# Windowed attention into a gated MLP on one core: gates without tanh, exponentials shifted by their bias, another first load and another order of the work

## The chip, the cores and the metric

The kernel runs on one core of a Trainium2 chip. The metric is the device time of one execution in microseconds (us); the number given for the kernel before is the median of three runs.

## The reference, cut to what matters

```python
q, k, v: (4, 8, 768, 64) float32          # batch, heads, sequence, head width
scores = q @ k^T / 8                      # per batch and head
keep   = (key < 4) | (0 <= query - key < 128)        # 4 sink keys and a window of 128
a      = softmax(where(keep, scores, -1e9))
x      = (a @ v) as (3072 tokens, 512)
h      = x @ w_in                         # 512 -> 2048
g      = h * sigmoid(1.702 * h)
out    = g @ w_out                        # 2048 -> 512, float32
```

## The kernel before

The tokens are cut into 24 blocks of 128 (six for each batch entry). A query block sees its own 128 keys up to the diagonal, those of the block ahead of it above the diagonal, and four sink keys. Two blocks make a group; there are 12 groups.

For a block, in order: the queries and keys are loaded by POOL's queue as float16 (`qkn`; block 0's first as float32 by SP's queue, `rawq` and `rawk`, and cast by ACT) and transposed (`qkT`; blocks 0 to 7 by PE into a `tq` tile, which DVE or ACT copies out, the later ones by a DMA transpose of SP's queue, both blocks of a group at once). PE makes the scores with the own keys (`own`), with those of the block before (`prv`) and with the sinks (`snk`). DVE packs `prv` into the masked half of `own`, takes the row maxima (`mx`), subtracts them (`e32`), and ACT takes the exponentials (`a16`). These are transposed, in blocks 0 to 3 by PE (`ta`, copied to `at`), later by a DMA transpose of SP's queue. POOL then splits them into `at` and `atp` by two selects. PE multiplies with the values (`av`), DVE divides by the sums (`xn`), and the result is transposed to `xT`, in blocks 0 to 3 by PE (`tx`), later by a DMA transpose. For a group, PE makes eight tiles of `h` (`hT`), ACT turns each into a gate (`gT`), and PE multiplies them with `w_out` (`o`, four parts for each of two token blocks), after which ACT or DVE copies to `osb` and SP's queue stores.

Group 0 is done apart. Its eight `hT` tiles are split by token block (four tiles each), so that the first four need block 0 alone. Its gates are made as (1 + tanh(0.851 h)) * h: ACT takes tanh, which lies in the same function table as exp, into `th`, and DVE multiplies. From group 1 on ACT takes the gate in one instruction, whose function lies in another table, so that ACT loads a table ahead of the gates and again ahead of the next exponentials.

In blocks 0 to 3 one half of each block (`nb` = 1) is not subtracted by DVE: ACT reads the scores in PSUM and subtracts the maximum by the bias of the exponential, head by head, in four instructions of 128 columns.

Nothing here is ordered by the Python loops. Every step is put into a list (`Plan.add`) with a cost, its dependences and the buffer rings that it takes and gives back (`RING`: among them two PSUM buffers `own`, three `mm`, which `tq`, `ta`, `tx`, `hT`, `o` and the `own` of blocks 1 and 3 share). `Plan.run` goes through the list with these costs, engine by engine, always taking the free step of the lowest key; the keys stand in the table `KEYS`. The order in which the steps are taken is the order of the instructions on each engine, and each engine works through its own in that order.

Of the kernel before, what the change touches and what calls it, by code (L numbers as in the profile page):

```python
# [11 lines left out]
FP32 = mybir.dt.float32  # L12
# [7 lines left out]
P = 128  # L20
# [11 lines left out]
    nb={0: 1, 1: 1, 2: 1, 3: 1},  # L32
# [3 lines left out]
    tanh=(0,),  # L36
# [6 lines left out]
    sel2=(),  # L43
    steady=8,
# [196 lines left out]
def kernel(  # L241
# [32 lines left out]
    plan = Plan(RING)  # L274

# [22 lines left out]

    def hw(key, cost, fn, xfer, **kw):
# [3 lines left out]
    o_bias0 = hw(-98, 0.4, lambda: nc.sync.dma_start(bias0, bias0_d.ap()), 0.1)  # L303
    o_later = hw(-97, 0.4, lambda: nc.sync.dma_start(later, later_d.ap()), 0.1)
    o_bias1 = hw(-96, 0.4, lambda: nc.sync.dma_start(bias1, bias1_d.ap()), 0.1)
    o_kept = hw(-94.5, 0.4, lambda: nc.sync.dma_start(kept, kept_d.ap()), 0.1)
    o_own = hw(-95, 0.4, lambda: nc.sync.dma_start(ownm, own_d.ap()), 0.1)
# [14 lines left out]
    def sw(key, cost, fn, xfer, **kw):  # L322
        return plan.add(POOL, key, cost, fn, xfer=xfer, post=2.6, **kw)
# [12 lines left out]

    def load_block(which, b, key, after=0.0):
        bb, r = divmod(b, 6)
        i = b % 2
        src = {"q": q, "k": k, "v": v}[which][bb, :, r * P : (r + 1) * P, :].rearrange("h s d -> s h d")  # L340
        if which == "v":
            return sw(key, 0.88, lambda: nc.gpsimd.dma_start(v65[:, b, :, 0:D], src), 1.0, deps=[z_1], after=after)  # L342
        w = "qk".index(which)
        buf = qkn[b // 2]
        if b in CFG["f32"]:
            raw = const.tile([P, H, D], FP32, name=f"raw{which}{b}")
            o_raw = hw(-120 + w, 0.4, lambda: nc.sync.dma_start(raw, src), 0.9)
            return plan.add(
                {DVE: 0.45, ACT: 0.6}, -95 + w, 0, lambda e: copy(e, buf()[:, i, w], raw), deps=[o_raw], take=[buf]
            )  # L350
        return sw(
            key, 0.88, lambda: nc.gpsimd.dma_start(buf()[:, i, w], src), 0.9,  # L352
            take=[buf], after=after,
        )
# [70 lines left out]
    o_qkt, o_ks, o_own_s, o_x = {}, {}, {}, {}  # L425

    for b in range(NBLK):
# [8 lines left out]
        if b in CFG["tq"]:  # L436
# [8 lines left out]
            for w in range(2):  # L445
                a = plan.add(
                    PE, K0 - 48 + w, 0.45 if b < 2 else 0.35, lambda w=w, f=t_qk: f(w), deps=[ld["qk"[w] + str(b)], o_ident],
# [37 lines left out]
        snk = ps("mi", (P, 4, 2, 4), FP32, f"snk{b}")  # L485
# [18 lines left out]
        if b in CFG["pemask"]:  # L504
            s_msk = plan.add(
                PE, K0 - 41, 0.9 if b == 0 else 0.43, lambda own=own, f=masks: f(own), deps=[o_bias0, o_identb] + (o_qkt[b] if b else []), take=own,
                slack=slack["s"],
            )
        s_own = None if both else plan.add(
            PE, K0 - 40, 0.5 if b < 2 else 0.24, lambda b=b, own=own, f=scores: f(own, b),  # L510
# [26 lines left out]
        if r > 0:  # L537

            def sinks(b=b, bb=bb, snk=snk):
                for j in range(4):  # L540
                    nc.tensor.matmul(snk()[:, j], qk_of(b)[:, j], ksb[:, bb, j], start=True, stop=True)

            s_snk = plan.add(PE, K0 - 40, 0.15, sinks, deps=([s_own] if b >= CFG['steady'] else []) + o_qkt[b] + [o_ks[bb]], take=[snk], give=[qkt[g]], slack=slack["s"])
# [69 lines left out]
        for l in range(2):  # L613
            if l >= 2 - nb:

                def exps(l=l, own=own, a16=a16, nbias=nbias):
                    for j in range(4):
# [7 lines left out]
                        ACT, K0 - 36.5, 1.02, exps, deps=[o_nb, z_a[b % RING["a16"]]],  # L625
# [18 lines left out]
        if r > 0:  # L644
# [9 lines left out]
            subs.append(plan.add(DVE, K0 - 38.7, 0.15, sub_s, deps=[top], take=[e32], give=[snk]))  # L654
# [99 lines left out]
        else:  # L754
            o_exp = plan.add(
                ACT, K0 - 36, 1.02, lambda a16=a16, e32=e32, w=w, f=exp: f(a16, e32, 0, w),
                deps=subs + zero, take=[a16], give=[e32], table="exp", slack=slack["e"],
            )
# [3 lines left out]
                deps=[o_exp], take=[at], give=[a16], xfer=1.35, post=0.8,  # L762
# [49 lines left out]
        if b in CFG["tx"]:  # L812
# [6 lines left out]
            o_tx = plan.add(PE, K0 - 28, 0.35, t_x, deps=norms, take=[tpx], give=[xn])  # L819
# [108 lines left out]
    order = plan.run()  # L928
    with tc.manual_schedule():
        for op in order:  # L930
            op.emit(op.on) if len(op.eng) > 1 else op.emit()
# [35 lines left out]
```

## Time and profile before

| | |
|---|---|
| median of the runs | 240.04 us (239.17 to 246.06, three runs) |
| profiled execution | 240.28 us, span 238.6 us |
| busy in the span | PE 216.5, DVE 141.2, ACT 133.8, POOL 114.2 us |
| chain that ended last | PE 76%, DMA 10%, DVE 7%, ACT 3% |
| moved by DMA | 33.38 MB, 126672 of 134152 packets under 512 bytes |

Busy times are those of one execution. Matmuls overlap each other, so PE's busy time says how long it had something in flight, not that it worked at its peak. The rows of a timeline give the start and the busy time in us, the engine, the line, the tiles with their shapes, the count, and in brackets how long the engine had been idle before and what ended that. SPq is the issue of DMAs by SP.

### The profile page before, as it was taken

What the parts mean: (1) busy time and instruction counts of PE and PEld (TensorE: products, weight loads), DVE (VectorE), ACT (ScalarE), POOL (GpSimd) and SP (SyncE); (2) the same over time, 40 slices, a digit from 0 to 9 for tenths busy, and PEclk for the clock granted to TensorE, in tenths of its full rate; (3) what the DMA queues carried; (4) which work ended last, traced back from release to release, by engine and by line L of the source; (5) the groups of instructions that cost most, each with busy time, mean ns of one, the idle gap of its engine ahead of it and who ended that gap; (6) DMA issues with size and microseconds to landing.
All of it is one profiled execution on the core that took longest, in us unless ns stands there. A gap on an engine that the chain in (4) does not pass through costs nothing.

```text
span 238.6 us, 5359 instructions
## 1 busy us (share of the span) xinstructions
PE 216.5 (91%) x2173; PEld 152.6 (64%) x2173; DVE 141.2 (59%) x344; ACT 133.8 (56%) x203; POOL 114.2 (48%) x130
## 2 busy tenths in 40 slices
PE   0368899899977999999999999999999999999994
PEld 0237598777436758648659568578577685685763
DVE  4279989827934556788598639767676571120000
ACT  3256686577226665737837565565666648351521
POOL 8878689199505618619708449644051210700000
PEclk9999769999999999999999999999999999999999
DMA  8999999999999997999999999999992223530202
GB/s 115 182 161 192 199 200 179 138 127 115 133 157 256 149 152 140 149 195 161 140 171 171 163 204 178 143 180 173 124 206 47 49 64 69 145 91 0 88 3 88
DMA packets 134152, 33.38 MB, mean 140 GB/s; under 512 B 126672, under 2 KB 131184, under 8 KB 134128
## 3 DMA queue, kind: packets, MB, share of 16 engines
q0 software_dynamic: 77024, 13.37, 73.8%
q1 hardware_dynamic: 57104, 19.67, 46.0%
q8 instruction: 17, 0.28, 0.5%
q14 instruction: 7, 0.06, 0.1%
HBM read 27.49 MB, written 6.29 MB: 142 GB/s over the span
## 4 chain that ended last, share of the span: by engine, by line
PE 76%; DMA 10%; DVE 7%; ACT 3%; SPq 1%; issue 1%; ACTq 0%; DVEq 0%
PE hT L852 33%; PE o L903 29%; DMA xT<-xn 7%; DMA bias<-cbias 3%; PE av L788 2%; PE av L792 2%; PE av L782 2%; PE own L522 2%; DVE mx L577 2%; DVE own L565 1%; DVE gT L873 1%; PE prv L522 1%; DVE xn L804 1%; DVE e L632 1%; PE ta L727 1%; PE tq L442 1%
## 5 line engine op out<-in xcount | busy, mean ns | idle before, releaser
L852 PE MATMUL hT<-xT,w_in 128*128 128x256 f16 (+1 forms) x832 | 93.5, 265 | 2.6 <-DMA xT<-xn 2.2
L903 PE MATMUL o<-w_out,gT 128*128 128x512 f16 (+1 forms) x400 | 90.2, 371 | 0.0
L852 PEld LDWEIGHTS <-w_in 128*128 128x128 f16 x832 | 74.6, 98 | 15.9 <-DMA xT<-xn 3.2
L882 ACT ACTIVATE gT<-hT 128x512 f16<-128x512 f32 x88 | 51.8, 597 | 41.7 <-PE hT L852 41.6
L676 POOL TENSOR_SCALAR_AFFINE_SELECT atp<-at 128x1024 f16<-128x1024 f16 (+1 forms) x23 | 22.5, 979 | 89.0 <-DMA at<-a 76.8
L903 PEld LDWEIGHTS <-gT 128*128 128x128 f16 x400 | 36.9, 98 | 35.0
L565 DVE COPY_PREDICATED own<-later,prv 128x512 f32<-128x512 uint16 x40 | 26.0, 691 | 18.0 <-PE prv L522 17.2
L577 DVE TENSOR_REDUCE mx<-own 128x4 f32<-128x512 f32 x48 | 31.1, 683 | 2.0 <-PE own L497 1.9
L664 ACT ACTIVATE a<-e 128x1056 f16<-128x1056 f32 (+3 forms) x27 | 24.5, 918 | 13.8 <-DVE e L632 6.8
L632 DVE TENSOR_TENSOR e<-own,mx 128x512 f32<-128x512 f32 x44 | 28.7, 682 | 0.5
L329 DVE COPY osb<-o 128x512 f32<-128x512 f32 (+1 forms) x7 | 4.6, 654 | 32.6 <-PE o L903 30.3
L333 ACT COPY osb<-o 128x512 f32<-128x512 f32 (+1 forms) x16 | 9.1, 572 | 25.8 <-PE o L903 25.8
L670 POOL TENSOR_SCALAR_AFFINE_SELECT at<-at 128x1024 f16<-128x1024 f16 (+1 forms) x23 | 22.4, 972 | 1.6
L342 POOL DMA_DIRECT2D v<-in_v_dram x24 | 21.7, 913 | 0.0
L352 POOL DMA_DIRECT2D qkn<-in_q_dram x23 | 21.0, 911 | 1.1 <-POOLq L948 0.8
L804 DVE TENSOR_TENSOR xn<-av,rcp 128x256 f16<-128x256 f32 x48 | 20.4, 425 | 1.7
L352 POOL DMA_DIRECT2D qkn<-in_k_dram x23 | 20.6, 898 | 0.3 <-DMA qkn<-in_q_dram 0.2
L803 DVE RECIPROCAL rcp<-av 128x4 f32<-128x4 f32 x48 | 8.4, 176 | 18.0 <-PE av L792 17.2
L788 PE MATMUL av<-v,at 128*128 128x65 f16 x192 | 17.5, 198 | 0.1
L788 PEld LDWEIGHTS <-at 128*128 128x128 f16 x192 | 14.9, 100 | 1.3
L442 PE MATMUL tq<-ident,qkn 128*128 128x128 f16 x64 | 7.6, 282 | 8.8 <-DMA ident<-cident 8.8
L792 PE MATMUL av<-v,atp 128*128 128x65 f16 x160 | 15.4, 197 | 0.0
(57 smaller groups left out, 180.7 us busy)
## 6 DMA issues: line engine op xcount, KB each, us to landing
out_dram<-osb SPq DMA_DIRECT2D x23, 256.0 KB, 2.6
v<-in_v_dram POOLq DMA_DIRECT2D x24, 128.0 KB, 6.2
qkn<-in_q_dram POOLq DMA_DIRECT2D x23, 128.0 KB, 6.3
qkn<-in_k_dram POOLq DMA_DIRECT2D x23, 128.0 KB, 5.7
w_in<-in_moe_w_in_dram POOLq DMA_DIRECT2D x4, 512.0 KB, 8.6
w_out<-in_moe_w_out_dram POOLq DMA_DIRECT2D x4, 512.0 KB, 11.2
at<-a SPq DMA_TRANSPOSE x20, 3.5
rawk<-in_k_dram SPq DMA_DIRECT2D x1, 256.0 KB
```

Source lines behind the costliest of these rows:

```text
L352: key, 0.88, lambda: nc.gpsimd.dma_start(buf()[:, i, w], src), 0.9,
L565: nc.vector.copy_predicated(out=own[l](), mask=later.unsqueeze(1).to_broadcast((P, 4, P)), data=prv[l]())
L577: lambda l=l, own=own, small=small: nc.vector.tensor_reduce(out=small[:, l], in_=own[l](), axis=AX.X, op=ALU.max),
L632: nc.vector.tensor_tensor(out=e32()[:, 512 * l : 512 * l + 512].rearrange("p (j s) -> p j s", j=4), in0=own[l](), in1=small[:, l].unsqueez ...
L664: nc.scalar.activation(out=a16()[:, lo:hi], in_=e32()[:, lo:hi], func=AF.Exp, scale=scale)
L670: nc.gpsimd.affine_select(out=dst()[:, lo : lo + n], in_=at()[:, lo : lo + n], pattern=[[0, n], [1, P]], compare_op=ALU.is_ge, fill=0.0, b ...
L676: nc.gpsimd.affine_select(out=dst()[:, lo : lo + n], in_=at()[:, lo : lo + n], pattern=[[0, n], [-1, P]], compare_op=ALU.is_gt, fill=0.0, ...
L788: nc.tensor.matmul(av()[:, j], ato()[:, c], v65[:, b, h], start=(r == 0), stop=(r == 0))
L804: nc.vector.tensor_tensor(out=xn()[:, i].rearrange("p (j l) d -> p l j d", l=2)[:, l], in0=av()[:, :, 0:D], in1=rcp.unsqueeze(2).to_broadc ...
L852: nc.tensor.matmul(ht()[:, n], w_in16[:, c, bass.ts(f, P)], xt[g]()[:, tok, c], start=(c == 0), stop=(c == 3))
L882: lambda fs=fs, cols=cols, gt=gt, ht=ht: nc.scalar.activation(out=gt()[:, fs[0] : fs[-1] + 1, cols], in_=ht(), func=AF.Gelu_apprx_sigmoid),
L903: nc.tensor.matmul(po(), gt()[:, F, bass.ts(t, P)], w_out16[:, F, cols], start=(F == 0), stop=(F == NF - 1))
```

## The change

- Group 0's gates are no longer made by tanh: ACT takes them by the gate function, in two batches of four, each after a table load.
- In blocks 0 to 3 both halves (`nb` = 2) are shifted by the bias of the exponentials. DVE's subtraction remains for the sinks.
- `rawq` is the first DMA of SP's queue and `rawk` one of ACT's queue, ahead of ACT's first table load. The constants follow on SP's queue (`ident`, `bias0`, `later`, `bias1`, `ownm`); `kept`, which no step of this configuration reads, is no longer loaded.
- Where the plan leaves PE idle within its first 45 us, products of a zero tile (`fill`, 128 x 256) into an unused part of the sinks' PSUM bank are put: 15 ahead of everything, 23 more in seven places up to block 4's sinks.
- Some costs given to the plan are altered, and the table `KEYS` is another, so that the order differs on every engine and in every group. On PE, `hT0_3` now stands right after half of block 3's transposes, ahead of block 3's scores, and the group 0 products with `w_out` end ahead of group 1's first `hT`. On ACT, the first four gates stand between the exponentials of block 1 and of block 2, the last four between those of block 3 and of block 4. On POOL, three loads more (block 8's keys, values and queries) are issued ahead of block 4's selects, and the four parts of `w_in` are its 3rd, 7th, 10th and 11th load, where they were the 4th, 12th, 14th and 18th. On SP, the order around group 2 is as before: block 4's and 5's `at`, `qkT` of blocks 8 and 9, `xT` of group 2, then block 6's and 7's `at`.

```diff
-    nb={0: 1, 1: 1, 2: 1, 3: 1},
+    nb={0: 2, 1: 2, 2: 2, 3: 2},
...
-    tanh=(0,),
+    tanh=(),
...
+    fill=(1.5, 45.0, 0.15, 0.11),
+    chain=99,
+    gap=3,
...
 KEYS = [ ... ]          # another table of the same kind
...
+    misc = psp.tile([P, 512], FP32, tag="mi", bufs=1, name="misc")
...
-    o_ident = hw(-99, 0.4, lambda: nc.sync.dma_start(ident, ident_d.ap()), 0.1)
...
-    o_kept = hw(-94.5, 0.4, lambda: nc.sync.dma_start(kept, kept_d.ap()), 0.1)
+    raw, o_raw = {}, {}
+    for b in CFG["f32"]:
+        for w, e in (("q", nc.sync), ("k", nc.scalar)):
+            src = {"q": q, "k": k}[w][b // 6, :, b % 6 * P : b % 6 * P + P, :].rearrange("h s d -> s h d")
+            raw[w, b] = const.tile([P, H, D], FP32, name=f"raw{w}{b}")
+            o_raw[w, b] = hw(-3000, 0.4, lambda dst=raw[w, b], src=src, e=e: e.dma_start(dst, src), 0.7)
+    o_ident = hw(-2000, 0.4, lambda: nc.sync.dma_start(ident, ident_d.ap()), 0.1)
...
+    fill = const.tile([P, 2 * P], FP16, name="fill")
+    z_f = plan.add(DVE, -2000, 0.1, lambda: nc.vector.memset(fill, 0.0))
...
-        snk = ps("mi", (P, 4, 2, 4), FP32, f"snk{b}")
+        snk = Buf("mi", lambda: misc[:, 0:32].rearrange("p (j l s) -> p j l s", l=2, s=4))
...
     order = plan.run()
+    idle, last = {}, 1.0
+    if CFG["fill"]:
+        lo, hi, rest, one = CFG["fill"]
+        for op in order:
+            if op.on == PE:
+                a, z = max(last, lo), min(op.start, hi)
...
+                idle[op] = max(0, int((z - a - rest) / (one if a > 6.0 else 2 * one)))
+                last = op.end
     with tc.manual_schedule():
         for op in order:
+            for n in range(idle.get(op, 0)):
+                nc.tensor.matmul(misc[:, 256:512], fill[:, 0:P], fill, start=True, stop=True)
             op.emit(op.on) if len(op.eng) > 1 else op.emit()
```

More of the change, by code (lines that the diff above doesn't have):

```diff
@@ L335, with load_one @@
     ld, qkn = {}, {}
+    late = []
     def load_block(which, b, key, after=0.0):
+        deps = [late[-CFG["gap"]]] if b >= CFG["chain"] and len(late) >= CFG["gap"] else []
+        op = load_one(which, b, key, after, deps)
+        if b >= CFG["chain"]:
+            late.append(op)
+        return op
+    def load_one(which, b, key, after, deps):
         bb, r = divmod(b, 6)
@@ L341, in load_block @@
         if which == "v":
-            return sw(key, 0.88, lambda: nc.gpsimd.dma_start(v65[:, b, :, 0:D], src), 1.0, deps=[z_1], after=after)
+            return sw(key, 0.88, lambda: nc.gpsimd.dma_start(v65[:, b, :, 0:D], src), 1.0, deps=[z_1] + deps, after=after)
         w = "qk".index(which)
@@ L345, in load_block @@
         if b in CFG["f32"]:
-            raw = const.tile([P, H, D], FP32, name=f"raw{which}{b}")
-            o_raw = hw(-120 + w, 0.4, lambda: nc.sync.dma_start(raw, src), 0.9)
             return plan.add(
-                {DVE: 0.45, ACT: 0.6}, -95 + w, 0, lambda e: copy(e, buf()[:, i, w], raw), deps=[o_raw], take=[buf]
+                {DVE: 0.45, ACT: 0.6}, -95 + w, 0, lambda e: copy(e, buf()[:, i, w], raw[which, b]),
+                deps=[o_raw[which, b]], take=[buf],
             )
@@ L352, in load_block @@
             key, 0.88, lambda: nc.gpsimd.dma_start(buf()[:, i, w], src), 0.9,
-            take=[buf], after=after,
+            take=[buf], after=after, deps=deps,
         )
@@ L423, in qk_of @@
         return qkt[b // 2]()[:, b % 2]
-    o_qkt, o_ks, o_own_s, o_x = {}, {}, {}, {}
+    o_qkt, o_ks, o_x, o_snk, o_sub = {}, {}, {}, {}, {}
     for b in range(NBLK):
@@ L446 @@
                 a = plan.add(
-                    PE, K0 - 48 + w, 0.45 if b < 2 else 0.35, lambda w=w, f=t_qk: f(w), deps=[ld["qk"[w] + str(b)], o_ident],
+                    PE, K0 - 48 + w, 0.45 if b < 2 and not CFG["fill"] else 0.27, lambda w=w, f=t_qk: f(w), deps=[ld["qk"[w] + str(b)], o_ident],
                     take=[tp], give=[qkn[g]],
@@ L505 @@
             s_msk = plan.add(
-                PE, K0 - 41, 0.9 if b == 0 else 0.43, lambda own=own, f=masks: f(own), deps=[o_bias0, o_identb] + (o_qkt[b] if b else []), take=own,
+                PE, K0 - 41, 0.9 if b == 0 and not CFG["fill"] else 0.43, lambda own=own, f=masks: f(own), deps=[o_bias0, o_identb] + (o_qkt[b] if b else []), take=own,
                 slack=slack["s"],
@@ L509 @@
         s_own = None if both else plan.add(
-            PE, K0 - 40, 0.5 if b < 2 else 0.24, lambda b=b, own=own, f=scores: f(own, b),
+            PE, K0 - 40, 0.5 if b < 2 and not CFG["fill"] else 0.24, lambda b=b, own=own, f=scores: f(own, b),
             deps=o_qkt[b] + [s_msk], take=[] if s_msk else own, give=[qkt[g]], slack=slack["s"] if s_msk is None else 0.0,
@@ L541, in sinks @@
                     nc.tensor.matmul(snk()[:, j], qk_of(b)[:, j], ksb[:, bb, j], start=True, stop=True)
-            s_snk = plan.add(PE, K0 - 40, 0.15, sinks, deps=([s_own] if b >= CFG['steady'] else []) + o_qkt[b] + [o_ks[bb]], take=[snk], give=[qkt[g]], slack=slack["s"])
+            s_snk = o_snk[b] = plan.add(PE, K0 - 40, 0.15, sinks, deps=([s_own] if b >= CFG['steady'] else []) + o_qkt[b] + [o_ks[bb]], take=[snk], give=[qkt[g]], slack=slack["s"])
         e32 = sb("e32", (P, 8 * P + 32), FP32, f"e32_{b}")
@@ L624 @@
                     plan.add(
-                        ACT, K0 - 36.5, 1.02, exps, deps=[o_nb, z_a[b % RING["a16"]]],
+                        ACT, K0 - 36.5, 1.14, exps, deps=[o_nb, z_a[b % RING["a16"]]],
                         take=[a16], give=[own[l]], table="exp",
@@ L652, in sub_s @@
                 )
-            subs.append(plan.add(DVE, K0 - 38.7, 0.15, sub_s, deps=[top], take=[e32], give=[snk]))
+            o_sub[b] = plan.add(DVE, K0 - 38.7, 0.15, sub_s, deps=[top], take=[e32], give=[snk])
+            subs.append(o_sub[b])
         w = 1024 + (32 if r > 0 else 0)
@@ L754 @@
         else:
[L755 to L758, printed above, removed]
+            cuts = [(0, w)] if not nb else ([(0, 512)] if nb == 1 else []) + ([(1024, w)] if w > 1024 else [])
+            o_exp = bexp + [
+                plan.add(
+                    ACT, K0 - 36, 0.2 + (hi - lo) / 1200, lambda a16=a16, e32=e32, lo=lo, hi=hi, f=exp: f(a16, e32, lo, hi),
+                    deps=subs + zero, take=[a16], give=[e32], table="exp", slack=slack["e"],
+                )
+                for lo, hi in cuts
+            ]
             o_at[0] = plan.add(
@@ L761 @@
                 lambda at=at, a16=a16, nch=nch: nc.sync.dma_start_transpose(at()[:, 0:nch], a16()[:, 0 : nch * P]),
-                deps=[o_exp], take=[at], give=[a16], xfer=1.35, post=0.8,
+                deps=o_exp, take=[at], give=[a16], xfer=1.35, post=0.8,
             )
@@ L928 @@
     order = plan.run()
+    idle, last = {}, 1.0
[4 more added lines that the diff above has]
+                a, z = max(last, lo), min(op.start, hi)
+                for b in o_snk:
+                    if o_snk[b].start < z and o_sub[b].done + 0.5 > a:
+                        a = max(a, min(z, o_sub[b].done + 0.5))
+                idle[op] = max(0, int((z - a - rest) / (one if a > 6.0 else 2 * one)))
+                last = op.end
     with tc.manual_schedule():
         for op in order:
+            for n in range(idle.get(op, 0)):
+                nc.tensor.matmul(misc[:, 256:512], fill[:, 0:P], fill, start=True, stop=True)
             op.emit(op.on) if len(op.eng) > 1 else op.emit()
```

13 lines of the change are left out of this document (8 added, 5 removed), and 63 rows, old and new, of the table KEYS.

## The prediction

> **What bounds the kernel now.** I read the page first, then busy times by stage, then the timeline of the first 75 us with the waits in its brackets.
>
> ```profile
> span 238.6 us, 5359 instructions
> PE 216.5 (91%) x2173; PEld 152.6 (64%) x2173; DVE 141.2 (59%) x344; ACT 133.8 (56%) x203; POOL 114.2 (48%) x130
> PE 76%; DMA 10%; DVE 7%; ACT 3%; SPq 1%; issue 1%; ACTq 0%; DVEq 0%
> ```
>
> PE is the engine of the whole, but an average hides where it is not. The stages (PE, PEld, DVE, ACT, POOL, granted clock, DMA share, GB/s):
>
> ```profile
> 0.00:13.40 13.40, 3.46 (x28) 2.45 (x29) 4.46 (x14) 4.24 (x6) 10.23 (x16) 1.00 1.39 149
> 13.40:46.90 33.50, 28.48 (x389) 23.48 (x389) 31.81 (x77) 22.38 (x54) 24.01 (x32) 0.90 1.78 180
> 46.90:73.25 26.35, 22.97 (x210) 14.17 (x208) 15.36 (x34) 14.44 (x19) 14.85 (x16) 1.00 1.63 128
> 73.25:91.00 17.75, 17.39 (x174) 12.35 (x175) 8.85 (x24) 11.29 (x16) 9.58 (x10) 1.00 1.47 199
> 91.00:235.30 144.30, 144.18 (x1377) 100.13 (x1375) 80.72 (x197) 81.17 (x111) 55.54 (x58) 1.00 0.96 126
> ```
>
> From 73.25 to 235.30 PE lacks 0.48 us in 162.05. So the end is fixed by when the first product of group 2's `hT` starts, at 73.25, and by what PE has done by then; behind it follow 162.05 us of PE, 3.3 us for the last copy and store, and 1.7 us outside the span (240.28 less 238.6). Ahead of it DVE is the full engine (31.81 of 33.50 from 13.40 on), and between 46.90 and 73.25 PE lacks 3.4 us. What holds 73.25:
>
> ```profile
> 37.50 1.10 ACT L664 ACTIVATE a<-e 128x1056 f16<-128x1056 f32 x1
> 38.63 10.69 SPq L761 DMA_TRANSPOSE at<-a  x2
> 47.87 1.09 POOL L676 TENSOR_SCALAR_AFFINE_SELECT atp<-at 128x1024 f16<-128x1024 f16 x1 [5.38 <-DMA at<-a]
> 50.06 0.90 POOL L342 DMA_DIRECT2D v<-in_v_dram  x1
> 53.54 0.92 POOL L352 DMA_DIRECT2D qkn<-in_q_dram  x1
> 58.81 4.12 SPq L461 DMA_TRANSPOSE qkT<-qkn  x1
> 63.02 1.69 SPq L830 DMA_TRANSPOSE xT<-xn  x1
> 69.85 0.23 PE L522 MATMUL own<-qkT 64*128 64x128 f16 x2 [1.35 <-DMA qkT<-qkn]
> 73.25 1.92 PE L852 MATMUL hT<-xT,w_in 128*128 128x256 f16 x16 [1.82 <-DMA xT<-xn]
> ```
>
> This is a train of transfers. Block 4's exponentials end at 38.60; their transpose lands 9.2 us later; POOL, which works in order, selects for 2.2 us and only then issues the last loads of blocks 8 and 9; these land for `qkT` at 58.81; `xT` of group 2 goes out behind `qkT` on SP's queue and lands 10.2 us later. PE waits at both ends of it.
>
> **The change part by part.** First the start, up to block 0's maxima.
>
> ```profile
> 0.80 0.44 SPq L347 DMA_DIRECT2D rawk<-in_k_dram  x1
> 3.82 0.62 ACT L333 CAST qkn<-rawk 128x512 f16<-128x512 f32 x1 [1.73 <-DMA rawk<-in_k_dram]
> 4.51 0.43 SPq L303 DMA_DIRECT2D bias<-cbias  x1
> 11.38 1.01 PE L489 MATMUL own<-bias,identb 128*128 128x512 bf16 x2 [1.14 <-DMA bias<-cbias]
> 13.40 1.29 DVE L577 TENSOR_REDUCE mx<-own 128x4 f32<-128x512 f32 x2 [1.92 <-PE own L497]
> ```
>
> Now `rawq` and `rawk` go out at about 0.8 on two queues, and `bias0` third on SP's queue, at about 2.0 instead of 4.51. It landed 6.9 us after its issue; the first load took 3.0 (0.80 to 3.82). So `bias0` is there between 5.0 and 8.8, and I take the middle, 6.9, since the queue is emptier but two large loads share the engines. Before, 2.0 us lay between the masks' start and the maxima; the new order has the keys' four transposes behind the masks and waits for their copy, some 0.6 each in the rows below, in place of others that took about 0.7: 2.5 us. So block 0's maxima start at T = 9.4 (7.5 to 11.3), 4.0 earlier. ACT's own DMA issue costs some 0.4 and is hidden: its casts wait for data anyway. The 15 fill products ahead of everything stand before any data; the other 23, where PE would not be idle, would cost 23 times the 0.11 of a 256-column product (the last fence's 3.49 for 32), 2.5 us, or twice that at half pace. Their cover is PE's wait on ACT's chain, worked out below; I take nothing.
>
> They might also quicken PE. The same four transposes take 0.60 early and 0.39 late, and 16 products of 128 columns 1.56 and 1.07:
>
> ```profile
> 15.12 0.60 PE L442 MATMUL tq<-ident,qkn 128*128 128x128 f16 x4
> 53.24 0.39 PE L442 MATMUL tq<-ident,qkn 128*128 128x128 f16 x4
> 32.44 1.56 PE L852 MATMUL hT<-xT,w_in 128*128 128x128 f16 x16
> 35.44 1.07 PE L852 MATMUL hT<-xT,w_in 128*128 128x128 f16 x16
> ```
>
> About a dozen such steps lie on the chain below, 0.2 us each: a gain between 0 and 2.4 us, of which I take none, because the fill stands thinnest where these steps are. The Trainium skill, "TensorE: Matmul & The Clock Gate", Part 4, says that transposes do not count as busy for the clock gate, which would leave the steps between fills slow; the slow early transposes agree with it, and no row here shows it by itself.
>
> **Then ACT**, by the rows of this stretch (mean ns between the bars):
>
> ```profile
> L632 DVE TENSOR_TENSOR e<-own,mx 128x512 f32<-128x512 f32 x8 | 5.5, 684 | 0.1
> L873 DVE SCALAR_TENSOR_TENSOR gT<-th,hT 128x512 f16<-128x512 f32 x8 | 5.4, 681 | 0.2 <-ACT th L866 0.2
> L866 ACT ACTIVATE th<-hT 128x512 f32<-128x512 f32 x8 | 4.8, 597 | 3.3 <-PE hT L852 2.2 <-DVE xn L804 1.0
> L664 ACT ACTIVATE a<-e 128x512 f16<-128x512 f32 x4 | 2.5, 631 | 1.3 <-DVE e L632 1.3
> 16.23 1.14 ACT L618 ACTIVATE a<-own,nb 128x128 f16<-128x128 f32 x4 [0.15 <-DVE nb L608]
> 107.02 0.59 ACT L333 COPY osb<-o 128x512 f32<-128x512 f32 x1 [2.31 <-PE o L903]
> 107.62 1.28 ACT L882 ACT_TABLE_LOAD   x1
> 108.92 1.57 ACT L882 ACTIVATE gT<-hT 128x512 f16<-128x512 f32 x3
> ```
>
> DVE loses four subtractions (2.7 us) and eight gate products (5.4), and takes over some ten copies from ACT, by ACT's 0.59 no more than 5.9: at least 2.2 us less, so it is no longer the full engine. ACT loses nothing for the gates (0.60 each for tanh, 0.60 for the gate row), pays 0.5 more for each of four halves (1.14 against 0.63), and loads its table four times more: 1.30 each with what lies around, 5.2. The work moves to ACT's order, counted from T: maxima and bias to T+1.5; eight exponentials 2.26; transposes and copy 1.2 (T+5.0); block 1's exponentials 2.5 (T+7.5); copies of `at` 0.8, `xT` and `qkT`, with PE's steps between (T+10.5); load 1.3; four `hT` tiles of 1.06 with PE's scores between them, the last gate at T+16.6; load 1.3; the exponentials of blocks 2 and 3, four times 1.14 and two of 0.23 (T+22.9); load 1.3; four gates behind PE's four tiles (T+27.5); load 1.3; block 4's exponentials 1.1: T+29.9. That is 39.3, where before it was 38.60 (T+25.2). The start's 4.0 us are spent: 4.7 go to loads, longer exponentials and the order.
>
> A rule speaks against this. The Trainium skill, "ScalarE: Activation LUTs", What ACT_TABLE_LOAD costs, counts 1.38 us of draining besides the load, 2.66 for every switch. By it four switches would cost 10.6 instead of 5.2. The rows 107.02 to 108.92 show copy, load and gate back to back, without it; I go by the rows and keep the rule as a rival.
>
> **Then the train.** With block 4's exponentials ending at 39.3, its transpose lands 9.2 us later (the row above) or 4.2 (the first pair below); I take the mean, 6.7, as POOL's loads are issued earlier.
>
> ```profile
> 84.57 1.73 SPq L761 DMA_TRANSPOSE at<-a  x1
> 88.75 1.09 POOL L676 TENSOR_SCALAR_AFFINE_SELECT atp<-at 128x1024 f16<-128x1024 f16 x1 [7.12 <-DMA at<-a]
> 81.31 6.41 DMA xT<-xn
> qkn<-in_k_dram POOLq DMA_DIRECT2D x23, 128.0 KB, 5.7
> 145.81 3.49 PE hT L852 x32
> 120.30 3.47 PE o L903 x16
> ```
>
> Selects 2.2: 48.2. Only two loads of block 9 are left instead of block 8's and 9's four and one of values: the last is issued 0.9 later and lands after 5.7: 54.8 (before 58.81). `xT` goes out 4.2 behind `qkT`, as before: 59.0. It lands 6.4 to 10.2 us later, 8.3 in the middle: **67.3** against 73.25.
>
> PE must be there too. Block 5's exponentials and the last of group 1's `xn` and `xT` put its first `hT` at about T+37, 46.4; eight tiles (64 products, 7.0), eight parts of `o` (32 products, 6.9) and some 2.5 of scores and values bring it to 62.8. So PE waits 4.5 us for the train, which stays the bound. Behind it PE has the same to do as before (block 8's sinks move ahead, 0.1). The sum: 240.28 - (73.25 - 67.3) = **234.3 us**. It is made against the profiled execution, 0.24 us over the median of 240.04, which is well inside the runs' own scatter; a measurement of this kernel tells about 2% from no change.
>
> Bounds: with T = 7.5, 4.2 and 6.4 the train lands at 61.0, and PE's path at 60.9 meets it: 228.0. With T = 11.3, 9.2 and 10.2 it lands at 73.6: 240.6. The likeliest case's own range is 229 to 238.
>
> **The rivals.** (1) The train does not move. For it: the stretch 13.40 to 46.90 already moves 180 GB/s, more than the two behind it on the mean, and three more loads are now issued towards its end, so both landings may be the slow ones (9.2, 10.2); and ACT arrives no earlier. With them, at T = 9.4: 39.3 + 9.2 + 2.2 + 0.9 + 5.7 + 4.2 + 10.2 = 71.7, time 238.7. Against it: POOL's loads go out earlier throughout.
>
> (1b) Every table switch costs a drain of about its own length besides the load, four times 1.36 us: with my landings `xT` is there at 72.7, time 239.7. The rows 107.02 to 108.92 speak against it; 0.02. It is the rule of the Trainium skill, "ScalarE: Activation LUTs", What ACT_TABLE_LOAD costs.
>
> (2) Slower: ACT and the three `mm` buffers in lock step. Block 3's scores hold two of the three until their exponentials, which stand last behind the first gates, the load and block 2's. Before, DVE's subtraction freed them. If each `hT` tile must wait for the gate of the one before, eight take 1.06 + 0.60 + 0.2 = 1.9 instead of 1.06, 6.7 us more; block 4's transpose then goes out at 46.0. With the slow landings `xT` is there at 78.4, time 245.4. From 45.2 on for that transpose the gain is gone at my landings; from about 50 it is slower by 2%. For it: ACT waits for `hT` even before (2.2 in its row), and `w_in`'s parts must land by T+15. Against: `w_in` is issued earlier, and five of the tiles in between are copied out by DVE.
>
> (3) The loads do not hurry, PE is quickened and the transfers land fast: 228 to 230, the lower bound above.
>
> **How the numbers follow.** Forecast, with the quick end (3) in it: 0.59; rival 1: 0.13, and 0.02 for the draining; rival 2, which grows beyond 245.4 if the next `xT` is late too: 0.26. Faster by over 2% means below 235.2, slower above 244.8. Of the forecast's case 0.09 lies above 235.2, of rival 2 0.03 below 244.8. Faster: 0.50; within: 0.27; slower: 0.23. The range, 229.0 to 247.0, takes in the bound of the quick case nearly and rival 2 with 1.6 us of a second late `xT`.
>
> **What would show it.** Right: block 0's maxima near 9.4; six table loads up to group 1's gates (two before); block 4's exponentials ending near 39 although the start is earlier; block 4's select near 46; `qkT`'s transpose near 55; group 2's `hT` at 67.3, PE waiting for `xT` just ahead of it, and 162 us of PE behind. Wrong at the start, if the maxima begin after 11.3; wrong in ACT's part, if block 4's exponentials end before 36 or after 43; wrong in the whole, if PE lacks more than 2 us after group 2's start, since I carry that stretch over unchanged.

## The result, and the profile after

The changed kernel takes 239.78 us (median of twelve runs, 237.49 to 242.64) against 240.44 for the kernel before beside it; the ratio is 0.994, with a 95% interval of 0.9912 to 0.9969. So it is a little faster, by 0.3 to 0.9%, where the forecast had 2.5% as the likeliest. (Every ratio leaves out executions over 1.5% above the fastest of the same kernel, while the times are medians of all; rows of the table below marked * are profiles of such executions.) The profiled execution took 239.70 us, 0.58 less than that of before.

The page of the changed kernel: span, busy times, the clock in 40 slices, and the chain that ended last.

```profile
span 238.0 us, 5442 instructions
PE 220.8 (93%) x2211; PEld 155.3 (65%) x2211; DVE 140.1 (59%) x341; ACT 138.2 (58%) x213; POOL 112.7 (47%) x128
PEclk9779999999979999999999999999999999999999
PE 56%; DMA 22%; DVE 13%; ACT 5%; issue 2%; POOL 1%; SPq 1%; ACTq 0%; POOLq 0%
```

The chain was 76% PE and 10% DMA before. It now is 56% and 22%: a part of the stretch that was PE's alone has become the transfers'. The busy times by stage (PE, PEld, DVE, ACT, POOL, granted clock, DMA share, GB/s):

```profile
46.50:68.50 22.00, 18.88 (x192) 12.71 (x192) 14.24 (x32) 13.76 (x20) 13.02 (x13) 1.00 1.88 153
68.50:91.00 22.50, 22.47 (x202) 16.00 (x201) 13.88 (x33) 12.38 (x17) 13.00 (x14) 0.92 1.25 169
91.00:120.50 29.50, 27.75 (x286) 18.66 (x285) 21.72 (x52) 17.63 (x23) 13.49 (x15) 1.00 1.48 149
120.50:234.60 114.10, 113.50 (x1060) 79.25 (x1059) 56.37 (x137) 63.38 (x88) 37.37 (x38) 1.00 0.82 117
```

Behind group 2's start PE lacks 0.03, 1.75 and 0.60 us, and one stage has a granted clock of 0.92. Before, PE lacked 0.48 there in all and the clock was 1.00. Right behind group 2's start the clock is 0.50, with PE busy throughout:

```profile
70.00:72.00 2.00, 2.00 (x11) 1.41 (x10) 0.14 (x1) 0.60 (x1) 1.03 (x1) 0.50 1.07 333
```

The timeline of the changed kernel at the places that the forecast named:

```profile
9.26 1.29 DVE L599 TENSOR_REDUCE mx<-own 128x4 f32<-128x512 f32 x2
38.17 1.09 ACT L687 ACTIVATE a<-e 128x1056 f16<-128x1056 f32 x1
39.28 6.54 SPq L788 DMA_TRANSPOSE at<-a  x2
47.35 1.59 POOL L699 TENSOR_SCALAR_AFFINE_SELECT atp<-at 128x1024 f16<-128x1024 f16 x1 [2.74 <-PE own L519]
56.82 3.67 SPq L483 DMA_TRANSPOSE qkT<-qkn  x1
60.59 1.27 SPq L857 DMA_TRANSPOSE xT<-xn  x1
68.53 4.45 PE L879 MATMUL hT<-xT,w_in 128*128 128x256 f16 x24 [1.82 <-DMA xT<-xn]
85.66 1.04 PE L879 MATMUL hT<-xT,w_in 128*128 128x256 f16 x8
103.89 2.78 PE L879 MATMUL hT<-xT,w_in 128*128 128x256 f16 x24 [0.19 <-DMA xT<-xn]
120.51 1.03 PE L879 MATMUL hT<-xT,w_in 128*128 128x256 f16 x8 [1.57 <-DMA xT<-xn]
172.66 1.05 PE L879 MATMUL hT<-xT,w_in 128*128 128x256 f16 x8 [0.52 <-DMA xT<-xn]
```

(The select at 47.35 waited for the landing of `at`; the row names PE, which had long been done.) Group 2's `hT` starts at 68.53 instead of 73.25: between these two executions 4.72 us were won there. Its first 24 products take 4.45 us, where they took 2.79 before (half clock), and at groups 4, 5 and 8 PE waits for `xT`, 2.28 us in all. At the end 0.65 us of the 4.72 is left.

One table holds most of what follows: where PE started `hT` of groups 2 and 3 and ended its last product, in the profiled executions (us).

| kernel | hT of group 2 | hT of group 3 | end of PE | behind group 2's start | behind group 3's start |
|---|---|---|---|---|---|
| before | 73.25 | 87.77 | 235.18 | 161.9 | 147.4 |
| before, second profile | 71.75 | 88.36 | 236.10 | 164.3 | 147.7 |
| before, first loads early | 67.65 | 84.60 | 232.10 | 164.4 | 147.5 |
| the same, block loads early too | 67.17 | 84.49 | 231.90 | 164.7 | 147.4 |
| the same, second profile | 67.88 | 84.20 | 231.77 | 163.9 | 147.6 |
| after | 68.53 | 85.66 | 234.53 | 166.0 | 148.9 |
| after, second profile * | 68.79 | 85.91 | 235.34 | 166.6 | 149.4 |
| after, third profile | 69.14 | 86.13 | 234.05 | 164.9 | 147.9 |
| after, gap filled | 69.54 | 84.99 | 231.46 | 161.9 | 146.5 |
| the same, second profile | 69.60 | 85.05 | 232.64 | 163.0 | 147.6 |
| after, gap filled, block loads early | 69.82 | 85.28 | 231.28 | 161.5 | 146.0 |
| after, no constant products * | 71.90 | 88.96 | 235.70 | 163.8 | 146.7 |
| the same, second profile | 68.95 | 84.58 | 230.84 | 161.9 | 146.3 |

### The profile page after: what moved, and what is told of

Its sections match the earlier page's. It is cut to its first block, busy times and chain, and to the rows that moved or that the text cites. A ratio compares the mean times of both kernels' runs of the same rounds, so it can differ in the third digit from the quotient of the medians.

```text
span 238.0 us, 5442 instructions
## 1 busy us (share of the span) xinstructions
PE 220.8 (93%) x2211; PEld 155.3 (65%) x2211; DVE 140.1 (59%) x341; ACT 138.2 (58%) x213; POOL 112.7 (47%) x128
## 4 chain that ended last, share of the span: by engine, by line
PE 56%; DMA 22%; DVE 13%; ACT 5%; issue 2%; POOL 1%; SPq 1%; ACTq 0%; POOLq 0%
PE hT L879 26%; PE o L930 21%; DMA xT<-xn 12%; DMA at<-a 4%; DMA qkT<-qkn 4%; DVE e L654 3%; DVE mx L599 2%; DVE xn L831 2%; DMA bias<-cbias 2%; ACT a L640 2%; PE av L815 2%; DVE own L587 1%; PE own L544 1%; ACT gT L909 1%; PE av L819 1%
## 5 line engine op out<-in xcount | busy, mean ns | idle before, releaser
L879 PE MATMUL hT<-xT,w_in 128*128 128x256 f16 (+1 forms) x832 | 95.2, 267 | 5.2 <-DMA xT<-xn 4.1
L909 ACT ACTIVATE gT<-hT 128x512 f16<-128x512 f32 x96 | 56.6, 597 | 56.4 <-PE hT L879 56.0
L930 PE MATMUL o<-w_out,gT 128*128 128x512 f16 (+1 forms) x400 | 89.2, 370 | 0.0
L654 DVE TENSOR_TENSOR e<-own,mx 128x512 f32<-128x512 f32 x40 | 26.5, 686 | 1.5
L347 ACT COPY osb<-o 128x512 f32<-128x512 f32 (+1 forms) x20 | 11.3, 565 | 25.2 <-PE o L930 16.1
L687 ACT ACTIVATE a<-e 128x1056 f16<-128x1056 f32 (+2 forms) x23 | 21.9, 973 | 5.9 <-DVE rcp L830 3.5
L374 POOL DMA_DIRECT2D qkn<-in_q_dram x23 | 20.5, 902 | 0.1
L815 PE MATMUL av<-v,at 128*128 128x65 f16 x192 | 16.9, 196 | 0.5 <-POOL at L693 0.5
```

The source lines that it names most:

```text
L654: nc.vector.tensor_tensor(out=e32()[:, 512 * l : 512 * l + 512].rearrange("p (j s) -> p j s", j=4), in0=own[l](), in1=small[:, l].unsqueez ...
L687: nc.scalar.activation(out=a16()[:, lo:hi], in_=e32()[:, lo:hi], func=AF.Exp, scale=scale)
L815: nc.tensor.matmul(av()[:, j], ato()[:, c], v65[:, b, h], start=(r == 0), stop=(r == 0))
L879: nc.tensor.matmul(ht()[:, n], w_in16[:, c, bass.ts(f, P)], xt[g]()[:, tok, c], start=(c == 0), stop=(c == 3))
L909: lambda fs=fs, cols=cols, gt=gt, ht=ht: nc.scalar.activation(out=gt()[:, fs[0] : fs[-1] + 1, cols], in_=ht(), func=AF.Gelu_apprx_sigmoid),
L930: nc.tensor.matmul(po(), gt()[:, F, bass.ts(t, P)], w_out16[:, F, cols], start=(F == 0), stop=(F == NF - 1))
```

## The experiments

**Is it the new order? (two runs)** The head of one kernel with the other's order from group 2's first `hT` on, by another table of keys:

```diff
-KEYS = [ ... the kernel's own ... ]
+KEYS = [ ... own ranks up to group 2's first hT, then those of the other kernel ... ]
```

The changed head with the order of before behind it:

> The changed kernel with the order of the kernel before for everything that stands behind group 2's first hT; all ahead of it is the changed kernel's own. Order theory (the new order of groups 3 to 9 brings new waits for xT): group 2's hT still starts near 68.5, the waits of 1.73 us near 118 and 0.68 us near 172 are gone, and PE needs about 163.7 us from group 2's hT to its end instead of 166.1 (162.05 and the 1.7 us of half clock stay), so the time is about 237.3 us, 1.2% under the kernel before. Clock theory alone (all of the loss is the half clock behind the wait at 66.7): the time stays near 239.7. Traffic theory (the transfers behind collide whatever the order): 239.7 too, with waits for xT of over 2 us at other places.

242.43 us against 241.35 for the kernel before, ratio 1.0018 (0.9981 to 1.0055). The mirror:

> The kernel before with the changed kernel's order behind group 2's first hT, the mirror of the first run. Order theory: hT of group 2 starts near 73.2 at full clock as before, but PE loses 2.4 us more behind it, in waits for xT: about 242.7 us, 1% over the kernel before. Clock theory alone: the 24 first products take 2.8 us as before and the time is that of the kernel before, 240.3. Traffic theory: 240.3 too.

243.69 us, ratio 1.0078 (1.0041 to 1.0114). The order theory asked for a gain in the first and a loss in the second. The second lost, as asked; the first can't be told from the kernel before, and against the changed kernel (0.994) it gained nothing. So the order of before is no cure. That an order fits only the head that it was made with would explain both, but no run shows it. The waits of the first hybrid behind 69 us, in total, times and longest:

```profile
PE hT L879 <- DMA xT<-xn: 2.5, 2, 1.4
PE av L815 <- POOL at L693: 1.9, 1, 1.9
PE hT L879 <- ACT gT L909: 1.1, 1, 1.1
```

**Is it the clock? (four runs)** 15 products of zeros where PE idles ahead of group 2's first `hT`:

```diff
+    idle[min(o_hT2, key=order.index)] = 15      # o_hT2: the eight hT steps of group 2
     with tc.manual_schedule():
```

The first try put them ahead of `hT2_0`, which in this order is not the first of the eight: they ran at 78.78, as 1.65 us of work for PE and nothing else.

> The changed kernel with 15 products of constants of zeros in the idle 1.8 us of PE just ahead of group 2's first hT, nothing else. Clock theory: the clock in the rows from 68.5 to 72 is 1.00 instead of 0.50 to 0.62, the first 24 products of hT take 2.8 us instead of 4.45, and the time falls by up to 1.7 us to about 238.0. If the wait for xT near 118 is set by a chain of transfers and not by PE, PE comes to it 1.7 us earlier and waits 1.7 us longer: the clock is full and the time stays at 239.7. If the idle time is not what lowers the clock, the 24 products stay near 4.4 us.

240.99 us, ratio 0.9959 (0.9921 to 0.9997); the 24 products took 4.45 us again. The changed kernel lay at 0.989 to 0.994 in three comparisons, so the misplaced 1.65 us may have cost 0.5 to 1.6; the intervals overlap. The same slip is in the run that joins it with the order of before:

> Both edits of the first and third run together: the changed kernel's head, 15 products of zeros ahead of group 2's hT, and the order of before behind it. If order and half clock are together all that the forecast missed, PE needs about 162.1 us behind group 2's hT as before, and with its start at 68.5 the time is 235.6 us, 2% under the kernel before. If something else of the changed kernel costs time behind that start (traffic), it stays over 237.

Its executions spread from 239.6 to 249.6 us and its ratio of 0.9968 (0.9914 to 1.0022) tells nothing apart. At the right place:

> The changed kernel with 15 products of zeros in PE's idle time just ahead of group 2's first hT, at the place that the third run missed (there they stood ahead of a later hT, at 78.8 us). Clock theory: the clock stays at 1.00 behind the gap and the first 24 products of hT take 2.8 us instead of 4.45. If PE bounds what follows, the time falls by 1.65 us against the changed kernel, to about 238; by the train theory it stays within 0.7 of it, since PE only comes sooner to the next wait for xT.

238.35 us against 241.29, ratio 0.9849 (0.9796 to 0.9903), and beside the unchanged kernel on another chip:

> The changed kernel with 15 products of zeros in the gap again, now beside the changed kernel itself on one chip. Clock theory: 1.65 us faster than the changed kernel, ratio to the kernel before lower by 0.007, group 2's first 24 products in 2.8 us and 162 us of PE behind their start. Train theory: as fast as the changed kernel within 0.5 us.

238.27 against 239.57 for the changed kernel and 241.71 for the one before, ratio 0.985 (0.979 to 0.9909) where the changed kernel has 0.9894 (0.9849 to 0.9938). Timeline and stage of the first of the two:

```profile
67.79 0.26 PE L564 MATMUL misc<-ksb,qkT 128*128 128x8 f16 x4
67.90 1.80 PE L974 MATMUL misc<-fill 128*128 128x256 f16 x15
69.54 2.78 PE L880 MATMUL hT<-xT,w_in 128*128 128x256 f16 x24
68.50:91.00 22.50, 22.50 (x230) 16.53 (x228) 14.70 (x36) 12.83 (x18) 13.24 (x14) 1.00 1.22 177
```

With the gap filled the clock is 1.00, the 24 products take 2.78 us, and group 3 starts 15.45 us behind group 2 instead of 17.13: the 1.68 us of the half clock. The half clock is shown as the cause of that delay. In the whole time it is less sharp: 0.985 and 0.9894, side by side, have intervals that overlap. The row of `hT` has no wait for `xT` left, so the zero products may themselves have held up its start; what it would be without that is not shown. PE then needs 161.9 us behind group 2's start (163.0 in the second run), as in the forecast. Of the waits for `xT` 0.3 us is left, and 1.4 in the second run; the changed kernel has 2.3 behind 84 us, and 1.5 in its third profile. In the first run PE came earlier and waited less, which is against the train theory: `xT` of group 5 was issued at 112.8 instead of 114.3. There the train hung on PE, as PE hangs on it. But 1.4 and 1.5 nearly meet, so how much of these waits goes with the half clock stays open.

**Does PE alone bound the stretch behind group 2's start?** The kernel before with less to do there; three of the four parts of the sum in group 2's `hT` are left out:

```diff
-                    for c in range(4):
+                    nk = 1 if g == 2 else 4
+                    for c in range(nk):
```

> The kernel before with 48 of the 64 products of group 2's hT left out (one of the four parts of the contraction stays), so PE has 48 x 0.1095 = 5.3 us less to do right behind 73.25, and nothing ahead of it is touched. Theory of the forecast (the stretch behind is bounded by PE alone): the end comes 5.3 us earlier, 235.0 us, ratio 0.978. Theory of the train (the transposes of xT keep their own pace; in the trace of before xT of group 3 landed at 87.7 and hT started at 87.8, of group 4 at 105.6 against 106.8, of group 8 at 171.6 against 171.8): PE only waits for xT instead, at groups 3, 4 and 8, and the time is over 238.5, ratio over 0.992.

241.36 us against 241.29, ratio 1.0017 (0.9989 to 1.0045). 5.3 us of PE's work are gone and nothing is won. Stages and waits of it:

```profile
72.00:74.00 2.00, 0.78 (x3) 0.20 (x2) 1.03 (x2) 1.54 (x4) 0.68 (x1) 0.70 0.68 240
74.00:76.00 2.00, 0.37 (x7) 0.38 (x8) 0.00 (x0) 0.00 (x0) 1.93 (x3) 0.50 1.21 326
76.00:78.00 2.00, 1.97 (x19) 1.24 (x16) 1.31 (x6) 1.08 (x2) 2.00 (x3) 0.50 1.26 208
78.00:80.00 2.00, 1.94 (x14) 1.26 (x15) 1.12 (x5) 1.22 (x3) 2.00 (x4) 0.59 1.87 119
72.13 0.38 PE L853 MATMUL hT<-xT,w_in 128*128 128x256 f16 x2 [0.85 <-ACT gT L883]
73.24 0.40 PE L782 MATMUL av<-vsb,at 128*128 128x260 f16 x1 [0.74 <-DMA at<-a]
75.63 0.23 PE L788 MATMUL av<-v,at 128*128 128x65 f16 x1 [1.99 <-POOL at L670]
```

PE waits at once for ACT's gates, for a transpose of `at` and for POOL's selects, 3.6 us, and behind these waits its clock is at half until near 79, at the cost of about 1.8 (3.9 busy us at 0.50 to 0.59). The stretch from group 2's start to group 3's then took 15.71 us (70.37 to 86.08) where it had taken 14.52: PE's work was not all that bounded it, and with a third of that work gone other chains held it at its length.

**How firm is 73.25?** Both kernels again, unchanged.

> The kernel before, unchanged, for a second profile. Group 2's hT started at 73.25 in its first profile, at 71.15 and 70.37 in the two kernels that share its head. If the forecast's base was an execution with a late train, hT starts near 71 here, and then either PE needs 162 us behind it and the time is 238, or (train theory) PE waits for xT later and the time stays near 240.3.

241.18 us, as the kernel before it is (ratio 0.9977, 0.9943 to 1.0011). Its first products of groups 2 and 3 and a wait between them, and the row of group 3 in the first profile of before:

```profile
71.75 2.79 PE L852 MATMUL hT<-xT,w_in 128*128 128x256 f16 x24 [0.39 <-DMA xT<-xn]
76.58 0.20 PE L788 MATMUL av<-v,at 128*128 128x65 f16 x1 [0.95 <-POOL at L670]
88.36 1.92 PE L852 MATMUL hT<-xT,w_in 128*128 128x256 f16 x16 [1.32 <-DMA xT<-xn]
```

```profile
87.77 1.92 PE L852 MATMUL hT<-xT,w_in 128*128 128x256 f16 x16 [0.36 <-DMA xT<-xn]
```

Group 2 starts 1.50 us earlier and PE ends 0.92 us later. The earlier start is given back in two waits: 0.95 us for POOL's select, which the first profile did not have, and 1.32 at group 3, which was there, at 0.36 us, in the trace that the forecast was made from. The base itself is loose: in the profiles of kernels with the head of before, group 2 starts at 70.37 (the run just above, which changes nothing ahead of it), 71.75 and 73.25; in those with the changed head, at 68.53, 69.14, 69.16 and 70.10. On the mean that is 2.6 us apart; the first pair, the latest of one and the earliest of the other, has 4.72.

> The changed kernel, unchanged, for a second profile on the chip of the other runs of this group. Group 2's hT at 68.5 to 70.2, its first 24 products in 4.45 us at half clock as in every kernel with this head so far, and 163.7 us (162.05 and the half clock's 1.65) to 166 behind it: 236 to 240. If the half clock was chance, the products take 2.8 us.

239.57 us, the half clock again (4.45 us).

> The changed kernel unchanged, as the yardstick of this group: group 2's first 24 products in 4.45 us at half clock, hT of group 3 near 85.8, waits of 1 to 3.5 us for xT behind it, 238 to 240.

239.40 against 240.74, ratio 0.9932 (0.9898 to 0.9967); the 24 products took 4.32 us. The half clock behind this gap stood in each of the six profiles of kernels with this head, all constant products and an unfilled gap.

**What do the first loads do alone?**

```diff
-            o_raw = hw(-120 + w, 0.4, lambda: nc.sync.dma_start(raw, src), 0.9)
+            e = nc.scalar if w else nc.sync
+            o_raw = hw(-120 + w, 0.4, lambda: e.dma_start(raw, src), 0.9)
+            raws.append(o_raw)
...
+    ahead = raws + [o_ident, o_bias0]
+    order = ahead + [op for op in order if op not in ahead]
```

> The kernel before with the first loads alone as in the changed kernel: raw queries first on SP's queue, raw keys on ACT's, then the identity and bias0, the others behind; ACT's and DVE's order stay as before. The maxima of block 0 start near 9.4 instead of 13.4. By the forecast's second step nothing here spends the 4 us, since the four extra table loads and the halves are not there: block 4's exps end 2 to 4 us earlier than 38.6, and group 2's hT starts 2 to 4 us earlier than 73.25. If PE bounds what follows, the time is 236.5 to 238.5; by the train theory, over 238.5.

238.52 us against 241.29, ratio 0.9867 (0.9824 to 0.991). Its maxima, block 4's exponentials and groups 2 and 3:

```profile
10.26 1.29 DVE L579 TENSOR_REDUCE mx<-own 128x4 f32<-128x512 f32 x2 [0.85 <-PE own L499]
33.45 1.08 ACT L666 ACTIVATE a<-e 128x1056 f16<-128x1056 f32 x1
67.65 2.79 PE L854 MATMUL hT<-xT,w_in 128*128 128x256 f16 x24
84.60 1.92 PE L854 MATMUL hT<-xT,w_in 128*128 128x256 f16 x16 [1.67 <-DMA xT<-xn]
```

Block 4's exponentials end at 34.53, 4.1 us earlier than before and 4.7 earlier than in the changed kernel. Group 2 starts at 67.65, group 3 3.2 us earlier than before, behind a wait for its `xT`; PE ends 3.1 us earlier. This edit alone is worth no less than the whole change.

**What do the constant products do?** The changed kernel without any:

```diff
-            for n in range(idle.get(op, 0)):
+            for n in range(0):
```

> The changed kernel without the constant products, all else in the same order. The forecast took nothing for them (bounded by 0 and 2.4 us of gain): the granted clock in the first 46 us falls from 0.93 to about 0.90, the products there take up to 2 us more in all, most of it in PE's waits; block 4's exps end within 1 us of 39.3 and the time is within 1 us of the changed kernel's.

239.01 us against 241.29, ratio 0.9808 (0.9753 to 0.9863), and beside the changed kernel:

> The changed kernel without any constant product, beside it on one chip. If the products carry a part of the gain: block 4's exps end 1 to 2 us later, hT of group 3 starts 1 to 3 us later and the time is 1 to 2.5 us over the changed kernel's. If they carry none, as the forecast took it: the same time within 0.7 us.

237.93 against 239.40 for the changed kernel; 0.9814 (0.9765 to 0.9863) against 0.9932. Its six runs lie between 236.0 and 242.8, so how much it wins is not settled; no run shows the products to help in the end. Two stages, block 4's exponentials, their transpose and the select behind it, and group 2 in the second run:

```profile
25.00:30.00 5.00, 2.55 (x46) 2.13 (x43) 4.14 (x14) 4.14 (x11) 5.00 (x8) 0.91 1.65 165
30.00:35.00 5.00, 5.00 (x52) 4.21 (x52) 3.33 (x7) 3.62 (x12) 2.57 (x3) 0.50 1.58 190
40.97 1.08 ACT L687 ACTIVATE a<-e 128x1056 f16<-128x1056 f32 x1
42.08 6.45 SPq L788 DMA_TRANSPOSE at<-a  x2
47.59 1.09 POOL L699 TENSOR_SCALAR_AFFINE_SELECT atp<-at 128x1024 f16<-128x1024 f16 x1 [0.20 <-DMA at<-a]
68.95 2.78 PE L879 MATMUL hT<-xT,w_in 128*128 128x256 f16 x24
```

Without them the clock falls by half at 30 to 35 us, and block 4's exponentials end at 42.05 instead of 38.03 in the changed kernel on the same chip. Yet group 2 starts at 68.95 against 69.14. The products win 4 us at block 4 and none at group 2: the transpose of `at` went out at 42.08 instead of 38.05, and the select behind it started at 47.59 instead of 46.38, so most of the 4 us was gone when it landed. In this execution PE waited 1.2 us ahead of block 8's scores and not at all ahead of group 2's `hT`, and its clock stayed full. The profile of the first run, an execution of 240.89 us, is another picture: the exponentials ended at 40.95, the select started at 49.31, group 2 at 71.90, PE waited 2.5 and 1.6 us there, and the half clock came. Each of these times is some 2.9 us later than in the changed kernel's third profile, so there nothing was given back.

**Do POOL's selects hold the train?** The loads of queries and keys of block 9 (in the kernel with the first loads alone: of blocks 8 and 9) ahead of block 4's selects:

```diff
+    early = [ld["k9"], ld["q9"]]
+    order = [op for op in order if op not in early]
+    order[order.index(o_sel4) : order.index(o_sel4)] = early
```

> The kernel with the first loads alone, and besides them the queries and keys of blocks 8 and 9 on POOL's queue ahead of block 4's selects instead of behind them, all else in the same order. POOL sat idle 5.8 us there, so the loads are issued some 5.7 us earlier and land near 47. If qkT of group 4 (55.92) and the xT of group 2 queued right behind it (59.93) wait for these loads, both come 2 to 5 us earlier and group 2's hT starts near 64; if xT waits for block 5's selects and norms, it comes within 1 us of 59.9 and hT within 1.5 us of 67.65. The time is then 235 to 238.5; if PE does not bound what follows, 238.5.

> The kernel before with the first loads early and the queries and keys of blocks 8 and 9 ahead of block 4's selects, beside the changed kernel on one chip. If the first loads alone carry the gain, it is as fast as the changed kernel or up to 2 us faster, 236.5 to 239; hT of group 2 near 67.2 at full clock, hT of group 3 near 84.5 behind a wait of 1.8 us for xT.

> The changed kernel with 15 products of zeros in the gap and the queries and keys of block 9 on POOL's queue ahead of block 4's selects. In the changed kernel POOL sat idle 2.7 us there. If qkT of group 4 (56.8) waits for these loads, its landing and the scores behind it come 2 to 4 us earlier and the wait of 2.5 us ahead of them goes; xT of group 2 still waits for block 5's norms near 60, so hT of group 2 starts within 1 us of 69.5, at full clock, and the time is that of the kernel with the gap filled, 1.65 us under the changed kernel, within 0.7.

With the first loads alone the move took `qkT` from 55.92 to 55.29 only; the two runs of it gave 237.39 us, ratio 0.9822 (0.977 to 0.9874), and 237.51, ratio 0.9883 (0.9844 to 0.9922). The changed kernel with the gap filled gave 236.87, ratio 0.9854 (0.9816 to 0.9893), where the changed kernel itself had 0.9932: of these kernels the one with the narrowest spread, 236.5 to 237.7, and faster than the changed kernel, as the gap filled alone was (0.985). Little of that can come from the loads. Their issue and time to landing, first there, then in the changed kernel:

```profile
qkn<-in_k_dram POOLq DMA_DIRECT2D x1, 128.0 KB, 12.0
qkn<-in_q_dram POOLq DMA_DIRECT2D x1, 128.0 KB, 11.9
```

```profile
qkn<-in_q_dram POOLq DMA_DIRECT2D x1, 128.0 KB, 5.5
qkn<-in_k_dram POOLq DMA_DIRECT2D x1, 128.0 KB, 5.5
```

Issued 6 to 8 us earlier (43.54 and 44.41 against 51.26 and 50.37), they took 12 us to land instead of 5.5, and `qkT` went out at 56.39 where it had been 56.82. So POOL's order does not hold this train; the landing of the transfers does. The 2 to 5 us that the expectations put on an earlier `qkT` did not come.

## Why the prediction was wrong, step by step

- **The start was right.** Maxima at 9.26 (said: 9.4), and 8.46 in the third profile.
- **ACT's part came out right, in part by luck.** Block 4's exponentials ended at 39.26 (39.3), 30.0 us behind the maxima (29.9, and 25.2 before), and six table loads stood up to group 1's gates (six). But the sum took nothing for the constant products, and without them the exponentials ended 31.5 and 32.6 us behind the maxima: ACT's chain was put 1.6 to 2.7 us too short, and the products made it up. No drain: in the changed kernel's rows the copy ends at 19.93, the load starts at 19.95 and the gate at 21.25. The Trainium skill, "ScalarE: Activation LUTs", What ACT_TABLE_LOAD costs, has 1.38 us more for each switch; no row shows it.

```profile
19.34 0.59 ACT L347 COPY qkT<-tq 128x512 f16<-128x512 f16 x1
19.95 1.28 ACT L909 ACT_TABLE_LOAD   x1
21.25 1.09 ACT L909 ACTIVATE gT<-hT 128x512 f16<-128x512 f32 x2
```

- **The constant products at nothing: not settled.** They do quicken the stretch ahead of block 4, by 2.9 and 4.0 us against the changed kernel's third profile (1.7 and 2.8 against its first). In one profile without them the train had given that back by group 2, in the other it had not; no run shows a gain at the end.
- **The train was 1.2 us off** (68.53 for 67.3): the landing of `at` took 8.1 us (said 6.7), the selects 3.1 (2.2), `qkT` went out at 56.82 (54.8), `xT` 3.8 behind it (4.2) and landed 7.9 later (8.3). But the links were not what the text made of them: loads issued earlier land no earlier. What rival 1 said of it, that landings grow with what is in flight, fits this; no run varies the traffic alone.
- **The step that failed is the last: "Behind it PE has the same to do as before".** PE had, and still the stretch took 166.0 us instead of 161.9. Two things were missing. The half clock behind PE's wait cost 1.68 us, which filling the gap took away; the forecast saw PE wait 4.5 us there (it was 2.0 in the first profile and 3.9 in the third) and put no price on the clock. And PE waited 2.28 us for `xT` at groups 4, 5 and 8, where it had waited 0.36 us in all before. These waits come and go: 1.5 to 2.8 us in the three profiles of the changed kernel, 0 to 1.4 with the gap filled. In the four profiles of kernels with the changed order whose clock stayed full there, the stretch took 161.5 to 163.0 us, near what was forecast.
- **The base was no firmer.** In kernels with the order of before the stretch can't be carried over from group 2's start: it took 161.9 us in one execution and 164.3 in another, and 163.9 to 164.7 with the first loads early, while from group 3's start on it took 147.4 to 147.7 in all five (149.4 where products of group 2 were left out). Where the start came forward, by 1.5 to 6 us, PE waited longer ahead of and at group 3. Counted from group 3's start, 87.77, the gain that the changed kernel reached is 2.11 us instead of 4.72, and 1.46 of it went again behind. That makes the 0.65. It is a count and not a cause, since the changed kernel does not wait at group 3.
- **The condition for being wrong was named and came true:** PE lacked 2.38 us behind group 2's start (said: over 2).
- **Rival 2 did not happen:** block 4's transpose went out at 39.28, not 46.
- **What stays open:** why 0.6 to 0.7 us at group 3's start (85.66 against 85.05 and 84.99 with the gap filled) grows to 1.9 and 3.1 at the end. The waits for `xT` come and go with it, and PE and the train wait for each other in turn, but no run takes this loop apart.

## What to carry to other kernels

A stretch in which an engine is busy all the time is not yet one that it bounds: before carrying it over from an earlier start, look for the first wait in it, however short (here 0.36 us at group 3), and count the gain from there. Even that is no full guard: with an earlier start, 0.95 us of wait came at a select where the first trace has none. Take a second profile of the kernel before, and move the base only by what both agree on: the start on which the sum rested differed by 1.5 us between two executions that ended within 0.4%, and by 2.9 over three. And where a change opens a gap ahead of products, price the clock behind the gap with it.

## What was not expected of the hardware

PE's granted clock fell to 0.50 behind gaps that were each under 3 us. In the changed kernel's first profile PE idled 0.19 and 1.82 us there, with 0.8 us of small products between, and the next 24 products took 4.45 us; in its third it idled 2.79 and 1.14. In the kernel before it idled 1.35 and 1.82, with some 1.6 us of products between, and they took 2.79. The Trainium skill, "TensorE: Matmul & The Clock Gate", Part 1, What's actually happening, says that the gate watches a free-running window of 3.4 us. The two cases, a fall behind the shorter idle time and none behind the longer, fit a window whose place in time matters, or a count of the work between the gaps, but no run shows either. The same page of the Trainium skill, under Why this matters for your kernels, advises against gaps over some 3 us; that would not have warned here.

And loads of 128 KB that took 5.5 us to land took 12 when they were issued 6 to 8 us earlier, right behind the issue of block 5's transpose of `at` (43.4).
